# A chunk's scalar steps on the vector engine: one tensor and per-partition scalars in place of two tensors, and four steps on key lengths moved to Pool

## The chip, the cores and the metric

The kernel runs on one core of a Trainium2 chip. The metric is the device time of one execution in microseconds (us), here the median of 3 executions. Five engines work beside each other, each through its own instructions in a fixed order: TensorE (PE in the profile), VectorE (DVE), ScalarE (ACT), GpSimd (POOL) and SyncE (SP), which here only issues transfers.

## The reference

Two layers follow each other. The first is a delta-rule recurrence for 4 batches of 8 heads, 768 steps and a head size of 48; the second is a feed-forward layer with a rational function over the 3072 resulting tokens.

```
def _attn_ref(q, k, v, beta):                      # q, k, v: (4, 8, 768, 48)
    k_n = k / (np.linalg.norm(k, axis=-1, keepdims=True) + 1e-06)
    for t in range(S):
        y[:, :, t] = einsum('bhd,bhde->bhe', q[:, :, t], state)
        v_old = einsum('bhde,bhd->bhe', state, k_n[:, :, t])
        state = state + beta[:, :, t] * einsum('bhd,bhe->bhde', k_n[:, :, t], v[:, :, t] - v_old)

def _moe_ref(x, w_in, w_out, a, b):                # x: (3072, 384), w_in: (384, 2048), w_out: (2048, 384)
    h = x @ w_in
    P = a[0] + a[1] * h + a[2] * h**2 + a[3] * h**3
    Q = 1.0 + abs(b[0]) * abs(h) + abs(b[1]) * h**2
    return (P / (Q + 1e-06)) @ w_out
```

## The kernel before

**Tiling.** The 768 steps are cut into 12 chunks of 64. Within a chunk the recurrence is written as products and a triangular solve, so that only the state passes from chunk to chunk. Products run in f16 with a high and a low part of each operand (three products stand for one in f32, `PASSES`), and so everything must be scaled by powers of two to keep within f16. Those scales are the small steps that this document is about: tensors of one element per partition (`128x1`), or of 2, 4 or 16.

**Stages.** First the weights are read and split (`load_in`, `load_out`; both call `to_f32`, which turns f64 words into f32 and has a clamp on Pool at L333). Beside it the first chunks' keys are prepared. Then a main loop goes over 12 chunks of 8 tiles: `hidden` (first product), `numerator` and `quotient` (the rational function: ACT, DVE and Pool on 128x512 tiles), `accumulate` (second product). Between the tiles stand pieces of the recurrence for later chunks (`attention`: `back` of the next chunk, `middle`, `front`, and `ahead` of the fourth).

**What sets the order.** The code is recorded in this order, and a scheduler then orders each engine's instructions by its own estimate of durations, with raised priority for some pieces. So a changed instruction also moves its neighbours. On the chip every engine works strictly in its order: an instruction that waits holds up all that stand behind it on its engine.

**The places that the change touches.**

- `scalars` (L775 to L811), 13 calls (chunk 0 in two halves): from a chunk's token scale it bounds the result of the rational function and makes six factors for each of the 8 tiles. Its steps are a chain on tile `kp` (and `sf`), one value per partition, mostly TENSOR_TENSOR on DVE; L801 and L802 are a logarithm and an exponential on ACT in the midst of it. Its last step, L810, writes `msc`, which the chunk's first `numerator` (ACT L843) needs.
- `scale_of` (L256): L261 and L262 on ACT make a root, then L263 on DVE cuts it to a power of two by AND with the constant tensor `tmask`.
- `scales` (L629): the scales of a chunk's queries and values, on tile `sc`; L640 and L644 are two-tensor steps.
- `keys_normalized` (L505), four chunks ahead: L511 sums squares on DVE into `nrm` (128x16), L513 clamps, ACT L514 and L515 make a root, DVE L516 to L520 correct and invert it, and Pool L521 scales the keys.
- `inverse` (L543): L554 copies a diagonal into `wt` before the triangular inverse, which runs on DVE from L565 to L598.
- `to_f32` (L325): Pool L333, a TENSOR_SCALAR with one operation, a maximum.

## Time and profile before

| what | value |
|---|---|
| median of 3 executions | 918.05 us (916.96 to 919.3) |
| the profiled execution's own time | 918.86 us |
| its span, first to last instruction | 917.1 us (1.8 us lie around it) |
| DVE busy | 842.7 us, 92% of the span, 1657 instructions |
| PE, POOL, ACT busy | 74%, 66%, 63% |
| mean granted TensorE clock | 0.931 |

How to read the profile: a group row has line, engine, operation, output<-input tile names and shapes, count, then busy time in us and the mean of one in ns, then the engine's idle time before these instructions and what ended it. A view of one line gives the shortest, the median and the longest duration instead. A timeline row has start and duration in us. A busy engine need not be at work: a row counts as busy from the instruction's start to its end, and what holds it up in between is not told apart.

### The profile page before, as it was taken

The numbers are of one execution on the slowest core, as the hardware profiler recorded it, in microseconds if no ns is written. First come the engines' busy times: TensorE is split into PE (matmuls) and PEld (weight loads), VectorE is DVE, ScalarE is ACT, GpSimd is POOL, SyncE is SP. The second block draws the span as 40 slices with busy tenths as digits, with TensorE's granted clock in tenths as the row PEclk, the third lists the DMA queues.
The fourth block names the chain that finished last, engine by engine and source line by source line (L and its number), as shares of the span: only waits on it lengthen the run. The fifth ranks groups of instructions, "written<-read, shape, count | busy, mean of one in ns | idle before, by whom it ended". The sixth has DMA issues, their size and how long they took to land.

```text
span 917.1 us, 23581 instructions
## 1 busy us (share of the span) xinstructions
PE 678.4 (74%) x9264; PEld 542.9 (59%) x9264; DVE 842.7 (92%) x1657; ACT 576.3 (63%) x1099; POOL 604.4 (66%) x479
## 2 busy tenths in 40 slices
PE   0321453877787886986798988888989798999785
PEld 0221443665575775765676876766767676766563
DVE  5999998887997999899999999999999999898976
ACT  4765776556466575666565766657657566677473
POOL 6866965636456376767677677676767665666754
PEclk9999996887989998999998989989989999999998
DMA  7969888679897779779268578468476662200000
GB/s 228 222 162 188 192 180 155 94 132 155 149 130 154 137 136 149 131 147 179 42 132 152 98 157 141 81 151 146 67 185 98 122 114 36 64 2 19 1 18 18
DMA packets 420110, 111.49 MB, mean 122 GB/s; under 512 B 361376, under 2 KB 416672, under 8 KB 420000
## 3 DMA queue, kind: packets, MB, share of 16 engines
q1 hardware_dynamic: 417824, 108.83, 63.5%
q8 instruction: 72, 1.18, 0.6%
q10 hardware_dynamic: 2176, 1.17, 0.4%
q14 instruction: 38, 0.31, 0.1%
HBM read 40.47 MB, written 26.23 MB: 73 GB/s over the span
## 4 chain that ended last, share of the span: by engine, by line
DVE 44%; issue 13%; DMA 11%; ACT 9%; PE 8%; POOL 8%; SPq 6%; POOLq 0%; DVEq 0%; ACTq 0%
DVE mw L868 5%; DVE mu L849 3%; DVE mg L867 3%; DVE mg L865 3%; DVE mu L850 3%; DVE z L238 3%; SPq L449 3%; PE po L888 2%; POOL mw L848 2%; DVE mu L872 2%; PE ph L826 2%; DMA wsi<-in_moe_w_in_dram 2%; DVE pr L586 2%; DMA tq<-xdq 2%; PE pg L417 1%
## 5 line engine op out<-in xcount | busy, mean ns | idle before, releaser
L888 PE MATMUL po<-w_out,mg 128*128 128x384 f16 x1152 | 225.9, 341 | 23.7 <-POOL mg L873 12.6
L826 PE MATMUL ph<-xT,w_in 128*128 128x256 f16 x1728 | 226.7, 284 | 19.7 <-DVE mu L850 19.3
L826 PEld LDWEIGHTS <-w_in 128*128 128x128 f16 x1728 | 173.2, 102 | 58.4 <-DVE mu L850 18.3
L873 POOL TENSOR_TENSOR mg<-mu,mr 128x512 f16<-128x512 f32 x96 | 131.2, 1367 | 76.5 <-DVE mu L872 34.6
L848 POOL TENSOR_TENSOR mw<-mw,mr 128x512 f32<-128x512 f32 x96 | 135.6, 1413 | 65.2 <-ACT mw L847 63.7
L888 PEld LDWEIGHTS <-mg 128*128 128x128 f16 x1152 | 112.3, 102 | 96.0 <-POOL mg L873 17.4
L417 PEld LDWEIGHTS <-kbd 128*128 128x128 f16 x1680 | 93.6, 119 | 45.4 <-issue 41.2
L843 ACT ACTIVATE mu<-ph,coef,msc 128x512 f32<-128x512 f32 x96 | 74.3, 774 | 44.8 <-DVE msc L810 15.4
L861 ACT ACTIVATE mr<-mw,msc 128x512 f32<-128x512 f32 x96 | 69.5, 726 | 50.2 <-POOL mw L848 49.8
L868 DVE SCALAR_TENSOR_TENSOR mw<-mw,msc,mg 128x512 f32<-128x512 f32 x96 | 96.3, 1003 | 1.2
L849 DVE TENSOR_TENSOR mu<-ph,mu 128x512 f32<-128x512 f32 x96 | 65.3, 681 | 16.8 <-ACT mw L847 14.2
L417 PE MATMUL pu<-z,ebd 128*128 128x48 f16 x1728 | 57.9, 188 | 25.8 <-DVE z L238 21.8
L417 PEld LDWEIGHTS <-ebd 128*128 128x128 f16 x1728 | 55.6, 100 | 30.9 <-issue 25.1
L870 POOL TENSOR_TENSOR mu<-mu,mw 128x512 f32<-128x512 f32 x36 | 48.0, 1332 | 38.1 <-DVE mw L868 26.3
L850 DVE SCALAR_TENSOR_TENSOR mu<-mu,msc,ph 128x512 f32<-128x512 f32 x96 | 71.4, 744 | 0.8
L867 DVE SCALAR_TENSOR_TENSOR mg<-mu,msc,mr 128x512 f16<-128x512 f32 x60 | 65.9, 1098 | 2.9 <-ACT mr L862 2.7
L847 ACT ACTIVATE mw<-ph,msc 128x512 f32<-128x512 f32 x96 | 66.5, 692 | 0.0
L845 ACT ACTIVATE mr<-ph,msc 128x512 f32<-128x512 f32 x96 | 65.6, 683 | 0.0
L872 DVE SCALAR_TENSOR_TENSOR mu<-mu,msc,mw 128x512 f32<-128x512 f32 x60 | 64.0, 1067 | 0.4
L417 PEld LDWEIGHTS <-wbd 128*128 128x128 f16 x1152 | 38.1, 103 | 43.0 <-issue 37.8
L862 ACT ACTIVATE mr<-mr 128x512 f32<-128x512 f32 x96 | 60.7, 633 | 1.5
L234 ACT ACTIVATE z<-pu,zmask 128x384 f16<-128x384 f32 x72 | 40.1, 579 | 32.4 <-PE pu L417 22.9
(216 smaller groups left out, 1491.4 us busy)
## 6 DMA issues: line engine op xcount, KB each, us to landing
wsi<-in_moe_w_in_dram SPq DMA_DIRECT2D x24, 256.0 KB, 5.3
xdk<-kn SPq DMA_DIRECT2D x12, 512.0 KB, 3.4
kbd<-tk SPq DMA_DIRECT2D x24, 256.0 KB, 5.1
gd<-g SPq DMA_DIRECT2D x24, 256.0 KB, 4.3
xdq<-kn SPq DMA_DIRECT2D x12, 512.0 KB, 4.5
wso<-in_moe_w_out_dram SPq DMA_DIRECT2D x32, 192.0 KB, 4.0
mbd<-mm SPq DMA_DIRECT2D x24, 256.0 KB, 4.9
wc<-img SPq DMA_DIRECT2D x24, 256.0 KB, 5.5
```

What stands on the lines that cost most here:

```text
L417: nc.tensor.matmul(dst[p][:, h], head(bd, lp, p * H + h), head(rt, rp, p * H + h), start=start and n == 0 and h == 0, stop=stop and n == l ...
L826: nc.tensor.matmul(ph[:, i], w_in[:, f2, wp, cc, i * P : (i + 1) * P], x[:, xp, cc], start=k == 0, stop=k == 3 * NCC - 1,)
L843: nc.scalar.activation(u, ph, AF.Identity, scale=A3, bias=a2)
L848: nc.gpsimd.tensor_add(w, w, z)
L849: nc.vector.tensor_mul(u, ph, u)
L850: nc.vector.scalar_tensor_tensor(out=u, in0=u, scalar=A1, in1=ph, op0=ALU.add, op1=ALU.mult)
L861: nc.scalar.activation(r, w, AF.Ln, bias=Q0)
L867: nc.vector.scalar_tensor_tensor(out=g[:, 0], in0=u, scalar=A0, in1=r, op0=ALU.add, op1=ALU.mult)
L868: nc.vector.scalar_tensor_tensor(out=w, in0=w, scalar=Q0, in1=g[:, 0], op0=ALU.add, op1=ALU.mult)
L872: nc.vector.scalar_tensor_tensor(out=u, in0=u, scalar=A0, in1=w, op0=ALU.add, op1=ALU.subtract)
L873: nc.gpsimd.tensor_mul(g[:, 1], u, r)
L888: nc.tensor.matmul(po[p], g[:, gp, i, p * P : (p + 1) * P], w_out[:, f2, wp, i], start=f2 == lo and i == 0 and k == 0, stop=f2 == hi - 1 a ...
```

## The change

- `scalars` no longer multiplies two tensors. Each step is a TENSOR_SCALAR: one tensor, and one or two operands that are one value per partition (or constants). The bound's two polynomials, until now done side by side on 128x4 and 128x2 tensors with the constant tensor `horner`, are done one value at a time. A call has 18 instructions on DVE instead of 19; two of them still have 2 elements, `L797` (a reciprocal) and the last `times`.
- `scale_of` and `scalars` cut to powers of two with an AND against a constant. `tmask` and `horner` and what fills them are gone.
- L640 and L644 in `scales` become TENSOR_SCALAR too.
- In `keys_normalized` the clamp, a product, a sum and a multiply-add (L513, L517, L518, L519) go from DVE to Pool. The two reciprocals stay on DVE, so the chain now goes DVE, Pool, ACT, ACT, DVE, Pool, Pool, Pool, DVE, Pool.
- The copy of L554 goes from DVE to ACT.
- Pool's clamp in `to_f32` has two operations, min with 3.0e38 and then max; the moved clamp has the same form.

```diff
+POWER = 0xFF800000
...
-    horner = cpool.tile([P, 2, 4], F32, name="horner")
...
+    def power_of_two(dst, src):
+        nc.vector.tensor_scalar(dst.bitcast(U32), src.bitcast(U32), POWER, None, op0=ALU.bitwise_and)
+
+    def times(dst, x, by, then=None):
+        if then is None:
+            nc.vector.tensor_scalar(dst, x, by, None, op0=ALU.mult)
+        else:
+            nc.vector.tensor_scalar(dst, x, by, then, op0=ALU.mult, op1=ALU.mult)
...
-        nc.vector.tensor_tensor(
-            out=dst.bitcast(U32), in0=lg.bitcast(U32), in1=tmask[:, :n], op=ALU.bitwise_and
-        )
+        power_of_two(dst, lg)
...
-        nc.gpsimd.tensor_scalar_max(a, a, keep)
+        nc.gpsimd.tensor_scalar(a, a, 3.0e38, keep, op0=ALU.min, op1=ALU.max)
...
-        nc.vector.tensor_scalar_max(ss, ss, 2.0 ** -94)
+        nc.gpsimd.tensor_scalar(ss, ss, 3.0e38, 2.0 ** -94, op0=ALU.min, op1=ALU.max)
...
-        nc.vector.tensor_mul(y1, y1, ss)
-        nc.vector.tensor_add(y0, y0, y1)
-        nc.vector.tensor_scalar(y0, y0, 1.0 / 32.0, 1e-6 / 16.0, op0=ALU.mult, op1=ALU.add)
+        nc.gpsimd.tensor_mul(y1, y1, ss)
+        nc.gpsimd.tensor_add(y0, y0, y1)
+        nc.gpsimd.tensor_scalar(y0, y0, 1.0 / 32.0, 1e-6 / 16.0, op0=ALU.mult, op1=ALU.add)
...
-        nc.vector.tensor_copy(wt[:, 0:256:17], bblk[:, c])
+        nc.scalar.copy(wt[:, 0:256:17], bblk[:, c])
...
-            nc.vector.tensor_max(sc[:, 1:2], sc[:, 1:2], fmax["v"])
+            nc.vector.tensor_scalar(sc[:, 1:2], sc[:, 1:2], fmax["v"], None, op0=ALU.max)
...
-        nc.vector.scalar_tensor_tensor(
-            out=sc[:, 5:6], in0=sc[:, 2:3], scalar=1.0 / 16.0, in1=sc[:, 3:4], op0=ALU.mult, op1=ALU.mult
-        )
+        times(sc[:, 5:6], sc[:, 2:3], 1.0 / 16.0, sc[:, 3:4])
...
-        nc.vector.tensor_mul(hm, wn, gm)
-        nc.vector.tensor_mul(t, horner[:, 0], hm.broadcast_to([P, 4]))
-        nc.vector.tensor_add(t, t, horner[:, 1])
-        nc.vector.tensor_mul(t[:, 0:2], t[:, 0:2], hm.broadcast_to([P, 2]))
-        nc.vector.tensor_scalar_add(t[:, 1:2], t[:, 1:2], 1.0)
-        nc.vector.reciprocal(t[:, 1:3], t[:, 1:3])
-        nc.vector.tensor_mul(t[:, 0:1], t[:, 0:1], hm)
-        nc.vector.tensor_mul(r, t[:, 0:4:3], t[:, 1:3])
-        nc.vector.tensor_add(gm, r[:, 0:1], r[:, 1:2])
-        nc.vector.tensor_add(gm, gm, m0)
-        nc.vector.tensor_mul(gm, gm, io)
+        times(hm, wn, gm)
+        def affine(dst, x, by, plus):
+            nc.vector.tensor_scalar(dst, x, by, plus, op0=ALU.mult, op1=ALU.add)
+        affine(top_, hm, m3, m2)
+        times(top_, top_, hm, hm)
+        affine(low, hm, b1, b0)
+        affine(low, low, hm, 1.0)
+        affine(one, hm, b0, 1.0)
+        nc.vector.reciprocal(kp[:, 5:7], kp[:, 5:7])
+        times(lin, hm, m1, one)
+        affine(gm, top_, low, lin)
+        nc.vector.tensor_scalar(gm, gm, m0, io, op0=ALU.add, op1=ALU.mult)
...
-        nc.vector.tensor_tensor(out=rk.bitcast(U32), in0=rk.bitcast(U32), in1=tmask[:, :1], op=ALU.bitwise_and)
+        power_of_two(rk, rk)
         nc.vector.reciprocal(sf[:, 1:2], rk)
-        nc.vector.tensor_mul(ikap, sf[:, 1:2], sf[:, 1:2])
-        nc.vector.tensor_mul(sf[:, 3:4], sf[:, 2:3], ikap)
-        nc.vector.tensor_mul(sf[:, 4:6], sf[:, 2:4], sf[:, 2:3].broadcast_to([P, 2]))
+        times(ikap, sf[:, 1:2], sf[:, 1:2])
+        times(sf[:, 3:4], sf[:, 2:3], ikap)
+        times(sf[:, 4:6], sf[:, 2:4], sf[:, 2:3])
```

Line numbers shift by up to three: what was L849, L850, L867 and L868 is L851, L852, L869 and L870. The steps of `scalars` now stand under the lines of their helpers: L252 is `power_of_two`, L257 and L259 `times` with one and with two factors, L789 `affine`. The scheduler moves neighbours in all engines' orders; three places matter for what follows.

DVE before, `scalars` of chunk 5 (tile `kp`), between the recurrence's splits (`z`, `xT`) and the tiles' own steps (`mg`, `mw`, `mu`):

```order
L786 RECIPROCAL kp_0_7772<-lgx_7707 128x1
L767 RECIPROCAL sf_7699<-sf_7699 128x1
L787 TENSOR_TENSOR kp_0_7772<-top,kp_0_7772 128x1
L789 TENSOR_TENSOR kp_0_7772<-horner,kp_0_7772 128x4
L790 TENSOR_TENSOR kp_0_7772<-kp_0_7772,horner 128x4
L791 TENSOR_TENSOR kp_0_7772<-kp_0_7772 128x2
L238 SCALAR_TENSOR_TENSOR xT_7697<-px_0_7712,sf_7699,xT_7697 128x3x128
L865 TENSOR_TENSOR mg_7843<-mu_7755,mr_7757 128x512
L792 TENSOR_SCALAR kp_0_7772<-kp_0_7772 128x1
L794 TENSOR_TENSOR kp_0_7772<-kp_0_7772 128x1
```

The same place now:

```order
L257 TENSOR_SCALAR kp_0_7755<-top,kp_0_7755 128x1
L233 SCALAR_TENSOR_TENSOR z_1_8096<-pu_0_7830,zmask,z_1_8096 128x384
L870 SCALAR_TENSOR_TENSOR mw_7667<-mw_7667,msc_6626,mg_7750 128x512
L789 TENSOR_SCALAR kp_0_7755<-kp_0_7755,coef 128x1
L233 SCALAR_TENSOR_TENSOR xT_7680<-px_0_7695,sf_7682,xT_7680 128x3x128
L789 TENSOR_SCALAR kp_0_7755<-kp_0_7755,coef 128x1 x2
L233 SCALAR_TENSOR_TENSOR z_1_8096<-pu_1_7831,zmask,z_1_8096 128x384
L259 TENSOR_SCALAR kp_0_7755<-kp_0_7755 128x1
```

The steps stay spread among the same kinds of neighbours; what changes is their kind.

Pool before, where chunk 7's keys are scaled (L521), ahead of a tile's sum (L848):

```order
L873 TENSOR_TENSOR mg_5809<-mu_5638,mr_5640 128x512
L249 TENSOR_SCALAR q_5495<-q_5495,sc_5876 128x768
L521 TENSOR_TENSOR k_5602<-k_5602,nrm_6129 128x768
L848 TENSOR_TENSOR mw_5801<-mw_5801,mr_5799 128x512
L230 TENSOR_SCALAR kn_120<-q_5495 128x2x8x48
```

Pool now, chunk 7 (L875, L850 and L524 were L873, L848 and L521):

```order
L875 TENSOR_TENSOR mg_5793<-mu_5622,mr_5624 128x512
L516 TENSOR_SCALAR nrm_6113<-nrm_6113 128x16
L520 TENSOR_TENSOR nrm_6113<-nrm_6113 128x16
L521 TENSOR_TENSOR nrm_6113<-nrm_6113 128x16
L522 TENSOR_SCALAR nrm_6113<-nrm_6113 128x16
L524 TENSOR_TENSOR k_5586<-k_5586,nrm_6113 128x768
L850 TENSOR_TENSOR mw_5785<-mw_5785,mr_5783 128x512
```

and chunk 10, which stands for most of the others:

```order
L516 TENSOR_SCALAR nrm_9560<-nrm_9560 128x16
L231 TENSOR_TENSOR gl_9194<-g_9189,gl_9194 128x768
L875 TENSOR_TENSOR mg_9240<-mu_9069,mr_9071 128x512
L520 TENSOR_TENSOR nrm_9560<-nrm_9560 128x16
L244 TENSOR_SCALAR q_8926<-q_8926,sc_9307 128x768
L521 TENSOR_TENSOR nrm_9560<-nrm_9560 128x16
L225 TENSOR_SCALAR kn_109<-q_8926 128x2x8x48
L522 TENSOR_SCALAR nrm_9560<-nrm_9560 128x16
L231 TENSOR_TENSOR kn_109<-q_8926,kn_109 128x2x8x48
L524 TENSOR_TENSOR k_9033<-k_9033,nrm_9560 128x768
```

Pool has four more instructions in each chunk, of which L520 needs ACT and DVE to have answered L516, and L524 needs DVE's second reciprocal. In chunk 7 (as in chunk 0) nothing else stands between them; in chunk 2 none stands between L516 and L520, in the others two to six do.

DVE before, the diagonal's copy (L554) in front of a tile's steps:

```order
L697 SCALAR_TENSOR_TENSOR v_5346<-v_5346,sc_5876,pk_1_7572 128x384
L554 COPY wt_122<-bblk 128x16
L868 SCALAR_TENSOR_TENSOR mw_7338<-mw_7338,msc_6643,mg_7563 128x512
L849 TENSOR_TENSOR mu_7552<-ph_7533,mu_7552 128x512
L872 SCALAR_TENSOR_TENSOR mu_7334<-mu_7334,msc_6643,mw_7338 128x512
```

ACT now, the same chunk's copy (L557) between two tiles' steps:

```order
L863 ACTIVATE mr_7537<-mw_7539,msc_6626 128x512
L227 CAST rr_7606<-v_5331 128x768
L864 ACTIVATE mr_7537<-mr_7537 128x512
L557 COPY wt_111<-bblk 128x16
L845 ACTIVATE mu_7663<-ph_7644,coef,msc_6626 128x512
```

The copy has left DVE's order and stands in ACT's.

More of the change, by code (lines that the diff above doesn't have):

```diff
@@ L153 @@
     nc.gpsimd.memset(consts[:, 2:3], 5.5 * LN2)
-    tmask = cpool.tile([P, 4], U32, name="tmask")
-    nc.gpsimd.memset(tmask, 0xFF800000)
     coef = cpool.tile([P, 12], F32, name="coef")
@@ L160 @@
     nc.scalar.activation(coef[:, 6:12], coef[:, 0:6], AF.Abs)
-    horner = cpool.tile([P, 2, 4], F32, name="horner")
-    nc.vector.memset(horner[:, 1], 0.0)
-    nc.vector.memset(horner[:, 1, 2:3], 1.0)
-    for i, (at, frm) in enumerate((((0, 0), 9), ((0, 1), 11), ((0, 2), 10), ((0, 3), 7), ((1, 0), 8), ((1, 1), 10))):
-        nc.vector.tensor_copy(horner[:, at[0], at[1] : at[1] + 1], coef[:, frm : frm + 1])
     a0, a1, a2, a3 = (coef[:, i : i + 1] for i in range(4))
-    m0, _, _, _, b0, b1 = (coef[:, i : i + 1] for i in range(6, 12))
+    m0, m1, m2, m3, b0, b1 = (coef[:, i : i + 1] for i in range(6, 12))
     bblk = cpool.tile([P, NCH, 16], F32, name="bblk")
@@ L782, in scalars @@
         kp = sb.tile([P, 10], F32, tag="kp", name=f"kp_{c}_{lo}", bufs=4)
-        gm, rk, ikap, hm = (kp[:, i : i + 1] for i in range(4))
-        t = kp[:, 4:8]
-        r = kp[:, 8:10]
+        gm, rk, ikap, hm, top_, low, one, lin = (kp[:, i : i + 1] for i in range(8))
         nc.vector.reciprocal(gm, d["lg"])
-        nc.vector.tensor_mul(hm, wn, gm)
-        nc.vector.tensor_mul(t, horner[:, 0], hm.broadcast_to([P, 4]))
-        nc.vector.tensor_add(t, t, horner[:, 1])
-        nc.vector.tensor_mul(t[:, 0:2], t[:, 0:2], hm.broadcast_to([P, 2]))
-        nc.vector.tensor_scalar_add(t[:, 1:2], t[:, 1:2], 1.0)
-        nc.vector.reciprocal(t[:, 1:3], t[:, 1:3])
-        nc.vector.tensor_mul(t[:, 0:1], t[:, 0:1], hm)
-        nc.vector.tensor_mul(r, t[:, 0:4:3], t[:, 1:3])
-        nc.vector.tensor_add(gm, r[:, 0:1], r[:, 1:2])
-        nc.vector.tensor_add(gm, gm, m0)
-        nc.vector.tensor_mul(gm, gm, io)
+        times(hm, wn, gm)
[10 more added lines that the diff above has]
+        nc.vector.tensor_scalar(gm, gm, m0, io, op0=ALU.add, op1=ALU.mult)
         nc.vector.tensor_scalar_max(gm, gm, 2.0 ** -60)
```

## The prediction

> **What bounds the kernel now.** I read the page's first part, then busy time by stage, because a mean over the span hides that the stages differ. The four stretches are the weights (to 150 us), the first chunks of the main loop, its steady part, and the end, where no keys are left to prepare.
>
> ```profile
> PE 678.4 (74%) x9264; PEld 542.9 (59%) x9264; DVE 842.7 (92%) x1657; ACT 576.3 (63%) x1099; POOL 604.4 (66%) x479
> core 0: us, PE busy (x) PEld busy (x) DVE busy (x) ACT busy (x) POOL busy (x), PEclk, DMA share, GB/s
> 0.00:150.00 150.00, 48.09 (x683) 40.47 (x683) 134.22 (x387) 93.66 (x231) 107.32 (x115) 0.98 0.86 192
> 150.00:350.00 200.00, 153.07 (x2310) 125.31 (x2310) 177.88 (x366) 118.10 (x221) 112.22 (x79) 0.87 0.81 138
> 350.00:750.00 400.00, 339.68 (x4770) 275.54 (x4771) 387.04 (x684) 258.49 (x463) 278.46 (x207) 0.93 0.70 127
> 750.00:918.00 168.00, 137.58 (x1508) 101.56 (x1504) 143.53 (x223) 106.02 (x187) 106.42 (x80) 0.97 0.13 25
> ```
>
> DVE bounds it: 89%, 89%, 97% and 85% of the four stretches, with no other engine over 85% in any. But busy is not at work. The next view shows DVE's small steps beside Pool in time order (start, duration).
>
> ```profile
> 448.69 1.71 POOL L873 TENSOR_TENSOR mg<-mu,mr 128x512 f16<-128x512 f32 x1
> 449.21 1.22 DVE L803 TENSOR_TENSOR kp<-kp,tmask 128x1 uint32<-128x1 uint32 x1
> 450.35 0.73 DVE L850 SCALAR_TENSOR_TENSOR mu<-mu,msc,ph 128x512 f32<-128x512 f32 x1
> 451.00 0.92 DVE L868 SCALAR_TENSOR_TENSOR mw<-mw,msc,mg 128x512 f32<-128x512 f32 x1
> ```
>
> L803 works on one element per partition and takes 1.22 us: it ends at 450.43, as Pool's L873 does (450.40). The same line's shortest, median and longest durations, and those of three comparable steps:
>
> ```profile
> L803 DVE TENSOR_TENSOR kp<-kp,tmask x13: 136/779/1771, 150.5 to 865.5; 128x1 uint32<-128x1 uint32 x13
> L378 DVE TENSOR_SCALAR vss<-wfs x8: 200/202/209, 88.2 to 151.9; 128x1 f32<-128x1 f32 x8
> L792 DVE TENSOR_SCALAR kp<-kp x13: 135/141/154, 145.3 to 857.4; 128x1 f32<-128x1 f32 x13
> L800 DVE TENSOR_SCALAR kp<-kp x13: 134/153/155, 149.6 to 864.8; 128x1 f32<-128x1 f32 x13
> ```
>
> A two-tensor step in SBUF takes 0.14 us or, behind Pool, up to 1.77 us. L792 and L800, with one tensor and constants, stand in the same chain and never exceed 0.155 us. L378, with one per-partition scalar, stays within 9 ns too. So what the change swaps is a kind that Pool stalls for one that it doesn't.
>
> **The change, part by part.** *Steps of `scalars`.* Busy time of the instructions on tile `kp`, by stage (ACT's are L801 and L802):
>
> ```profile
> core 0: us, DVE busy (x) ACT busy (x), PEclk, DMA share, GB/s
> 0.00:150.00 150.00, 3.59 (x14) 0.20 (x1) 0.98 0.86 192
> 150.00:350.00 200.00, 20.97 (x56) 3.51 (x11) 0.87 0.81 138
> 350.00:750.00 400.00, 41.27 (x102) 9.02 (x24) 0.93 0.70 127
> 750.00:918.00 168.00, 18.02 (x51) 5.68 (x14) 0.97 0.13 25
> ```
>
> At 0.149 us each (between L792's and L800's medians) these would be 2.1, 8.3, 15.2 and 7.6 us; the rest, 1.5 + 12.6 + 26.1 + 10.4 = 50.6 us, is stall. Other two-tensor steps that change:
>
> ```profile
> L263 DVE TENSOR_TENSOR sf<-lgx,tmask 128x1 uint32<-128x1 uint32 x12 | 5.6, 465 | 0.6 <-ACT lgx L262 0.6
> L644 DVE SCALAR_TENSOR_TENSOR sc<-sc 128x1 f32<-128x1 f32 x12 | 4.8, 401 | 0.0
> L263 DVE TENSOR_TENSOR sc<-lgq,tmask 128x2 uint32<-128x2 uint32 x12 | 4.3, 356 | 0.0
> L807 DVE TENSOR_TENSOR sf<-sf 128x2 f32<-128x2 f32 x13 | 4.2, 319 | 0.1
> ```
>
> The first two hold 12 x (465 - 149) + 12 x (401 - 149) = 6.8 us of stall. The last two keep 2 elements. No row has such a step with one tensor; it lies between L800 (1 element, free) and L513 below (16 elements, one tensor and constants, mean 416 though its neighbour L517 takes 212). I leave their stall in place; were it gone, 12 x 207 + 13 x 170 = 4.7 us of DVE time more would be won.
>
> The Trainium skill, "Advanced Engine Details and Errata", section "VectorE Performance Modes", says that a one-tensor instruction uses both read ports where source and destination lie in SBUF and their outermost non-unit dimension is even, and that the second port is shared with GpSimd. By that rule 1-element steps are free of Pool and 2-element ones are not, as I took them; the trace bears out the first (L792, L800) and L513's spread fits the second.
>
> *What a stall that goes is worth.* The next two-tensor instruction inherits part of it. At 449.21, without L803's 1.07 us of stall, L850 (which reads PSUM) would end about 450.0, and L868 would wait for Pool until 450.4 and end near 451.1 instead of 451.92: 0.8 us of 1.07. I take 0.8, so 40.5 us on `kp` and 5.4 us on the two others.
>
> *The price of a per-partition scalar.* L378 against L792 gives 61 ns for one; for two the bounds are 61 and 122 ns. Per call six steps have one and six have two, 0.73 to 1.10 us, over 13 calls 9.5 to 14.3 us; L640 and L644 add 1.5 us. One instruction fewer per call gives 1.9 us back. Sum 9 to 14, taken as 12 us.
>
> *Steps that leave DVE.*
>
> ```profile
> L513 DVE TENSOR_SCALAR nrm<-nrm 128x16 f32<-128x16 f32 x12 | 5.0, 416 | 0.0
> L517 DVE TENSOR_TENSOR nrm<-nrm 128x16 f32<-128x16 f32 x12 | 2.5, 212 | 0.0
> L518 DVE TENSOR_TENSOR nrm<-nrm 128x16 f32<-128x16 f32 x12 | 4.5, 378 | 0.0
> L519 DVE TENSOR_SCALAR nrm<-nrm 128x16 f32<-128x16 f32 x12 | 3.3, 271 | 0.0
> L554 DVE COPY wt<-bblk 128x16 f32<-128x16 f32 x12 | 9.2, 770 | 0.0
> ```
>
> That is 24.5 us off DVE. On ACT the copy should cost what L514 does on the same shape (212 ns, 2.5 us in all), beside an engine that is 63% busy: nothing. Pool's price for 16 elements lies between a memset of one and a TENSOR_SCALAR of 192:
>
> ```profile
> L153 POOL MEMSET consts<- 128x1 f32 x1 | 0.1, 98 | 0.0
> L177 POOL TENSOR_SCALAR bblk<-bblk 128x192 f32<-128x192 f32 x1 | 0.4, 399 | 0.3 <-issue 0.3
> L514 ACT ACTIVATE nrm<-nrm 128x16 f32<-128x16 f32 x12 | 2.5, 212 | 2.1 <-DVE nrm L513 2.0
> L333 POOL TENSOR_SCALAR wao<-wao,gate 128x192 f32<-128x192 f32 x32 | 28.7, 906 | 14.6 <-ACT wao L332 8.0 <-DVE gate L602 6.4
> ```
>
> 48 x 98 to 399 ns is 5 to 19 us on Pool, 66% busy. Its own time is covered; its waits are not. In order, Pool must now stand at L520 until ACT and DVE have answered L516, and the tile steps L848 and L873 stand behind. Before, DVE's chain for chunk 7 ran from 386.96 to Pool's start at 397.40:
>
> ```profile
> 386.96 0.16 DVE L513 TENSOR_SCALAR nrm<-nrm 128x16 f32<-128x16 f32 x1
> 397.40 1.48 POOL L521 TENSOR_TENSOR k<-k,nrm 128x768 f32<-128x768 f32 x1 [0.88 <-DMA wbd<-wc]
> ```
>
> Chunk 7 has no other Pool work in between, so up to 10.4 us; elsewhere in the main loop two to five instructions stand between L516 and L520. I charge 5 us in all; the bounds are 0 and the rival below.
>
> *Pool's clamp.* L333 (192 elements, one operation) takes 906 ns, L177 (192 elements, two operations, multiply and add) 399. Whether min and max run at that pace no row shows: from no gain to 56 x 0.4 = 22 us of Pool time in the first 150 us. DVE's steps there stall behind it, but transfers are also 86% busy. I take 4 us.
>
> *Sum by stage.* DVE time won is 0.8 x stall + what leaves - scalars' price; the 6.8, 24.5 and 12 us spread by calls:
>
> - 0 to 150: 1.2 + 0.2 + 2.7 - 0.9 = 3 us, half of it paid out, 2 us.
> - 150 to 350: 10.1 + 1.4 + 8.9 - 3.0 = 17 us.
> - 350 to 750: 20.9 + 2.8 + 12.9 - 5.6 = 31 us, at 97% DVE paid out at 0.9, 28 us.
> - 750 to the end: 8.3 + 1.0 + 0 - 2.5 = 7 us.
>
> In the second and fourth stretch DVE idles 11 and 15%, so the gain must lie on a chain that others wait for. It does:
>
> ```profile
> ACT kp L801 <- DVE kp L800: 19.6, 6, 7.3
> ACT mu L843 <- DVE msc L810: 15.4, 7, 5.5
> ```
>
> ACT waits 35 us on this very chain, the second time to begin a chunk's tiles. I pay out 0.7: 17 us. Together 2 + 28 + 17 = 47 us. Against it, the same Pool work in a shorter span meets DVE more often. Four big groups show what stalls remain, L850 (PSUM input, 744) being their floor:
>
> ```profile
> L868 DVE SCALAR_TENSOR_TENSOR mw<-mw,msc,mg 128x512 f32<-128x512 f32 x96 | 96.3, 1003 | 1.2
> L867 DVE SCALAR_TENSOR_TENSOR mg<-mu,msc,mr 128x512 f16<-128x512 f32 x60 | 65.9, 1098 | 2.9 <-ACT mr L862 2.7
> L872 DVE SCALAR_TENSOR_TENSOR mu<-mu,msc,mw 128x512 f32<-128x512 f32 x60 | 64.0, 1067 | 0.4
> L850 DVE SCALAR_TENSOR_TENSOR mu<-mu,msc,ph 128x512 f32<-128x512 f32 x96 | 71.4, 744 | 0.8
> ```
>
> They hold 25 + 21 + 19 = 65 us; 5% denser is 3 us. Net: 47 + 4 - 5 - 3 = 43 us. From the profiled execution's 918.86 us that is 875.9, and 0.8 us less against the median: **875 us**.
>
> **The rivals.**
>
> *DVE is the clock everywhere.* Stalls pay in full, in all stages: 50.6 + 6.8 + 24.5 - 9 + 8 for the clamp = 81 us, 837 us. For it: ACT's waits on DVE's chain. Against it: DVE idles 22 us in 150 to 350. Chance 0.11.
>
> *The stall moves on.* Pool and DVE's two-tensor work exclude each other; if that sharing is itself full, the next two-tensor instruction takes the whole wait over. Then only the unstalled time that leaves counts, 60 x 0.16 (L513 unstalled, above) = 10 us, against 12 us for scalars, and 4 us from the clamp: 916 us, or 911 if a tenth of the 57 us of stall still pays. Against it: Pool is only 66% busy, so a wait often ends with Pool idle. Chance 0.08.
>
> The Trainium skill, "VectorE: DVE Perf Modes", section "Rules for kernel authors", says to minimize the count of operations rather than fuse. By count alone `scalars` goes from 19 to 18 and time would hardly move, as in this rival; the spread of L803 speaks against it.
>
> *Scalars collide too.* If a per-partition scalar's read is blocked as a second tensor's is, only the AND steps with constants win (L803 12 x 0.6 and L263 3.8 us) and what leaves DVE: 0.8 x 11 + 24.5 - 12 = 21 us, paid at 0.8 = 17, less 4 for clamp, queue and denser Pool together: 905 us. Against it: L378, 8 of 8 free, though only in the weights. Chance 0.07.
>
> *Pool's queue becomes the clock.* Nine chunks prepare keys inside the main loop. If Pool's stand at L520 and L524 holds the tiles up by 6 us in each, 54 us replace the 5 charged and the time is 875 + 49 = 924 us; it decides against the change from about 5 us per chunk. For it: chunk 7's order and its 10.4 us. Against it: Pool idles 210 of the 600 us from 150 to 750, and work stands in between elsewhere. Chance 0.07.
>
> **How the numbers follow.** The forecast has 0.67, its own range 855 to 895: the 58 us of DVE time paid out at 0.6 or in full give 887 or 864, and I leave 8 us each way for the scheduler's new neighbours. To leave out no more than 2 in 10 I take 845 to 905. Within 0.3%, 2.8 us, counts as no change, about what this kernel's measurement can tell. Faster: 0.67 + 0.11 + 0.07 + most of 0.08 = 0.91, of which I move 0.02 to the others; same 0.04; slower 0.07.
>
> **What would show it.** Right: the steps at the new lines of `times` and `affine` at 0.14 to 0.27 us without a tail over 0.5; DVE's busy time down to about 785 us; ACT's waits for L801 and L843 on DVE halved; L868 and L867 a little longer than 1003 and 1098. Wrong: a tail in those steps (scalars collide); L868 and L867 at 1250 or more (the stall moves on); Pool idle before L520 or L524 by over 40 us with the tiles' ACT steps waiting on Pool (the queue). A time under 845 would say that the stalls cost more than their own length, one over 905 that what DVE gave up another engine took.

## The result, and the profile after

The changed kernel takes 896.29 us (median of 4, 895.7 to 898.5) against 917.89 us for the kernel before (916.96 to 919.3): ratio 0.977, 95% interval 0.975 to 0.979. It is 21 us faster; 43 us were forecast. The profiled execution took 898.5 us, with a span of 896.8. Its mean granted TensorE clock was 0.881, against 0.931 before, but another execution of the changed kernel at 0.951 took 895.7 us: the clock does not explain the missing 22 us.

The busy times and the shares of the chain that ended last, on the page of the changed kernel:

```profile
PE 675.2 (75%) x9264; PEld 540.7 (60%) x9264; DVE 798.7 (89%) x1576; ACT 575.2 (64%) x1111; POOL 603.1 (67%) x526
DVE 39%; PE 14%; DMA 12%; issue 10%; SPq 9%; ACT 9%; POOL 7%; ACTq 0%; POOLq 0%; DVEq 0%
```

The same chain on the page of the kernel before, which the prediction did not use:

```profile
DVE 44%; issue 13%; DMA 11%; ACT 9%; PE 8%; POOL 8%; SPq 6%; POOLq 0%; DVEq 0%; ACTq 0%
```

DVE's busy time fell by 44.0 us (842.7 to 798.7), not by 58, and 21 of the 44 reached the end. The chain had hinted at the second: with DVE busy for 92% of the span, only 44% of the chain was DVE's.

The new small steps in the changed kernel, grouped by line and shape (busy us, mean ns | idle before):

```profile
L257 DVE TENSOR_SCALAR sf<-sf 128x2 f32<-128x2 f32 x13 | 7.9, 608 | 0.1
L789 DVE TENSOR_SCALAR kp<-kp,coef 128x1 f32<-128x1 f32 x39 | 7.5, 241 | 0.2
...
L252 DVE TENSOR_SCALAR sc<-lgq 128x2 uint32<-128x2 uint32 x12 | 5.6, 467 | 0.0
L801 DVE TENSOR_SCALAR kp<-kp,coef,top 128x1 f32<-128x1 f32 x13 | 3.5, 267 | 0.2
...
L257 DVE TENSOR_SCALAR kp<-top,kp 128x1 f32<-128x1 f32 x13 | 2.6, 197 | 0.0
...
L252 DVE TENSOR_SCALAR kp<-kp 128x1 uint32<-128x1 uint32 x13 | 1.9, 143 | 0.1
```

One element: 143 ns with a constant, some 200 with one per-partition scalar, 267 with two; none of them exceeds 0.28 us. Two elements: 608 and 467 ns on average (319 and 356 before), with medians of 228 and 160. Ten of these 25 take over 0.5 us, and each of the ten ends 23 to 28 ns after an instruction of Pool: they stall behind Pool. L797, a reciprocal of two elements in the same chain, does not: 147 to 166 ns in all 13. The four big groups that hold the remaining stall:

```profile
L870 DVE SCALAR_TENSOR_TENSOR mw<-mw,msc,mg 128x512 f32<-128x512 f32 x96 | 101.0, 1052 | 1.1
L852 DVE SCALAR_TENSOR_TENSOR mu<-mu,msc,ph 128x512 f32<-128x512 f32 x96 | 70.7, 736 | 0.7
L874 DVE SCALAR_TENSOR_TENSOR mu<-mu,msc,mw 128x512 f32<-128x512 f32 x60 | 67.8, 1130 | 0.4
L869 DVE SCALAR_TENSOR_TENSOR mg<-mu,msc,mr 128x512 f16<-128x512 f32 x60 | 65.0, 1084 | 0.2
```

L870 and L874 grew by 49 and 63 ns a piece, L869 shrank by 14.

Where the gain arose is read from the start of `msc` (L810, now L812), which ends each chunk's chain. In the timeline of the kernel before, chunks 1 and 9:

```profile
243.38 0.20 DVE L810 TENSOR_TENSOR msc<-tab,sf 128x48 f32<-128x48 f32 x1
...
775.25 0.20 DVE L810 TENSOR_TENSOR msc<-tab,sf 128x48 f32<-128x48 f32 x1
```

and of the changed kernel:

```profile
232.18 0.19 DVE L812 TENSOR_TENSOR msc<-tab,sf 128x48 f32<-128x48 f32 x1
...
762.68 0.40 DVE L812 TENSOR_TENSOR msc<-tab,sf 128x48 f32<-128x48 f32 x1
```

11.2 us are won by chunk 1. From there to chunk 9, 531.9 us became 530.5: in the stretch that holds the 97% busy stage, where most of the gain was forecast, next to nothing came. The end brings the rest. DVE did get faster between these two marks: its busy time fell from 508.8 to 485.6 us. But its idle time rose from 23.1 to 44.9 us. The 23 us became waiting. The stage from 350 to 750 us shows the same, where DVE's 387.04 us of the prediction's view are now:

```profile
core 0: us, PE busy (x) PEld busy (x) DVE busy (x) ACT busy (x) POOL busy (x), PEclk, DMA share, GB/s
350.00:750.00 400.00, 342.89 (x4875) 277.15 (x4876) 367.92 (x664) 257.29 (x470) 290.93 (x229) 0.93 0.70 128
```

### The profile page after: what moved, and what is told of

Same layout as the page of the kernel before. It is cut to its first block, busy times and chain, and to the rows that moved or that the text cites. A ratio compares the mean times of both kernels' runs of the same rounds, so it can differ in the third digit from the quotient of the medians.

```text
span 896.8 us, 23571 instructions
## 1 busy us (share of the span) xinstructions
PE 675.2 (75%) x9264; PEld 540.7 (60%) x9264; DVE 798.7 (89%) x1576; ACT 575.2 (64%) x1111; POOL 603.1 (67%) x526
## 4 chain that ended last, share of the span: by engine, by line
DVE 39%; PE 14%; DMA 12%; issue 10%; SPq 9%; ACT 9%; POOL 7%; ACTq 0%; POOLq 0%; DVEq 0%
DVE mw L870 4%; PE ph L828 4%; PE po L890 4%; DVE mg L869 4%; PE pg L420 3%; DVE mu L874 3%; DVE w_out L344 3%; DVE mu L851 3%; POOL mg L875 3%; DVE mu L852 3%; DVE mg L867 3%; SPq L452 2%; SPq L118 2%; DMA gb<-gd 2%; DMA k<-in_k_dram 2%
## 5 line engine op out<-in xcount | busy, mean ns | idle before, releaser
L875 POOL TENSOR_TENSOR mg<-mu,mr 128x512 f16<-128x512 f32 x96 | 131.6, 1371 | 72.6 <-DVE mu L874 49.5
L850 POOL TENSOR_TENSOR mw<-mw,mr 128x512 f32<-128x512 f32 x96 | 138.0, 1438 | 47.4 <-ACT mw L849 46.8
L845 ACT ACTIVATE mu<-ph,coef,msc 128x512 f32<-128x512 f32 x96 | 74.4, 775 | 51.5 <-DVE msc L812 19.8
L870 DVE SCALAR_TENSOR_TENSOR mw<-mw,msc,mg 128x512 f32<-128x512 f32 x96 | 101.0, 1052 | 1.1
L851 DVE TENSOR_TENSOR mu<-ph,mu 128x512 f32<-128x512 f32 x96 | 65.6, 683 | 22.8 <-ACT mw L849 19.6
L852 DVE SCALAR_TENSOR_TENSOR mu<-mu,msc,ph 128x512 f32<-128x512 f32 x96 | 70.7, 736 | 0.7
L874 DVE SCALAR_TENSOR_TENSOR mu<-mu,msc,mw 128x512 f32<-128x512 f32 x60 | 67.8, 1130 | 0.4
L849 ACT ACTIVATE mw<-ph,msc 128x512 f32<-128x512 f32 x96 | 66.7, 694 | 0.0
L869 DVE SCALAR_TENSOR_TENSOR mg<-mu,msc,mr 128x512 f16<-128x512 f32 x60 | 65.0, 1084 | 0.2
L420 PEld LDWEIGHTS <-wbd 128*128 128x128 f16 x1152 | 36.3, 100 | 35.4 <-issue 33.4
L420 PE MATMUL pg<-tk,kbd 128*128 128x64 f16 x576 | 39.2, 241 | 17.9 <-DVE w_out L344 6.7
```

The lines of the kernel that those rows point to most:

```text
L420: nc.tensor.matmul(dst[p][:, h], head(bd, lp, p * H + h), head(rt, rp, p * H + h), start=start and n == 0 and h == 0, stop=stop and n == l ...
L845: nc.scalar.activation(u, ph, AF.Identity, scale=A3, bias=a2)
L850: nc.gpsimd.tensor_add(w, w, z)
L851: nc.vector.tensor_mul(u, ph, u)
L852: nc.vector.scalar_tensor_tensor(out=u, in0=u, scalar=A1, in1=ph, op0=ALU.add, op1=ALU.mult)
L869: nc.vector.scalar_tensor_tensor(out=g[:, 0], in0=u, scalar=A0, in1=r, op0=ALU.add, op1=ALU.mult)
```

## The experiments

Two theories stood at first. **Order**: the forms won what was forecast, and the scheduler's new order gave half of it back. **Stall**: the order matters little; the stall moves on to the next two-tensor step, or freed time turns into waiting. To tell them apart, a program's instructions were held in the order of another: every instruction is tied to the one ahead of it on its engine, without a wait. Steps that a run adds, and that the other program lacks, are not held; the scheduler puts them where they fit. The cuts of code below are shortened to what the edit does.

```diff
+for keys in order.values():                  # one list per engine, from the other kernel
+    both = [mine[k] for k in keys if k in mine]
+    for first, then in zip(both, both[1:]):
+        tc.add_manual_dep(then, first.name, NO_SYNC, reason="hold")
```

All ratios below are to the kernel before, measured beside each run, and a difference in us is a difference of ratios times 917.9 us; with intervals of about 0.003 either way, two or three us between two kernels mean nothing. "DVE busy" is the page's figure.

### The forms alone, in the order of before

```diff
-nc.vector.tensor_tensor(out=rk, in0=rk, in1=tmask[:, :1], op=ALU.bitwise_and)
+nc.vector.tensor_scalar(rk, rk, POWER, None, op0=ALU.bitwise_and)
-nc.vector.tensor_mul(ikap, sf[:, 1:2], sf[:, 1:2])
+nc.vector.tensor_scalar(ikap, sf[:, 1:2], sf[:, 1:2], None, op0=ALU.mult)
...
```

> The kernel before with every engine's instructions held in its own order; only the one-element two-tensor steps of scale_of, scalars and finish_q (the ANDs, hm, gm, ikap, sf, sc) take one tensor and per-partition scalars; the four-element Horner rows and all else stay. Theory O (the scheduler's new order cost what the forms had won): the forms alone win well here, 20 us or more, 898 or less. Theory S (the stall moves on to the next two-tensor step, or the freed time turns into waiting): 5 to 12 us, 906 to 913, with the stall of the big steps (mw, mg, mu) up by a third of what the small ones lose and DVE's idle time up by another third.

Measured: ratio 0.9971 (0.9949 to 0.9992), 2.7 us faster, and DVE busy 830.5 us. Less than even theory Stall expected; in before's order the forms do not win what was forecast, so Order falls there.

### Two-tensor forms back, in the order of after

The reverse of that edit, for all the small steps of the changed kernel:

```diff
-nc.vector.tensor_scalar(dst, x, by, plus, op0=ALU.mult, op1=ALU.add)
+nc.vector.scalar_tensor_tensor(out=dst, in0=x, scalar=by, in1=plus, op0=ALU.mult, op1=ALU.add)
...
```

> The changed kernel with every engine held in its own order; only the small steps' form goes back to two tensors, one for one (mult and add with a tensor as the second operand, AND with a tensor mask). Theory O: the forms are worth 25 us or more in a fixed order, so 921 or more. Theory S: they are worth about half the change, 8 to 15 us, so 904 to 911.

Measured: 0.9930 (0.9905 to 0.9956), 910.8 us; DVE busy 822.1. So in the order of after the forms are worth 14.9 us (within 3), about 0.64 of the 23.4 us of DVE time. The two-tensor steps in this run:

```profile
L295 DVE SCALAR_TENSOR_TENSOR kp<-kp,coef 128x1 f32<-128x1 f32 x39 | 14.1, 383 | 0.3
L295 DVE SCALAR_TENSOR_TENSOR kp<-kp,coef,top 128x1 f32<-128x1 f32 x13 | 6.9, 527 | 0.2
```

383 and 527 ns are L789's 241 and L801's 267 in the changed kernel.

As this run and the changed kernel have the same 1576 DVE instructions in the same order, each can be compared with itself (and likewise before with the run ahead). Sums of durations and of idle time ahead, in us:

```
                              two forms -> one form   before -> one form
changed small steps (206)        91.3 -> 52.5            86.5 -> 58.2
next instruction behind one     +11.2  (163)            +12.4  (177)
second behind one                +4.3  (133)             +4.8  (144)
all others                       -0.6                    -2.2
DVE's idle time                 +12.4                    +3.8
```

Part of the stall does move on: the next two instructions take over 15.5 of 38.8 us (40%) in the one order and 17.2 of 28.3 us (61%) in the other. All instructions further behind together take over nothing.

### Before's order for the changed program, and the reverse

```diff
-hold(changed, order_of(changed))
+hold(changed, order_of(before))     # and the reverse: hold(before, order_of(changed))
```

> The changed kernel, but every instruction that it shares with the kernel before keeps that kernel's order on its engine; the steps of the chain, the four length steps on Pool and the copy on ACT are put in where they fit. Theory O: the gain forecast comes back, 875 to 885. Theory S: the order is not what matters, 892 to 902.

Measured: 0.9870 (0.9834 to 0.9906), 905.0 us.

> The reverse of the last: the kernel before with every shared instruction held in the order of the changed kernel. Theory O: the new order alone costs 10 to 20 us, 928 to 938. Theory S: no more than 4 us from the kernel before, 914 to 922.

Measured: 0.9962 (0.9935 to 0.9990), 913.0 us. Neither supports Order for the whole span: the changed program in before's order is slower, not faster, and lies even above the range of Stall; the kernel before in the new order lies within 4 us of itself. By stretch (start of `msc` in chunks 1 and 9, one profiled execution each) it is not so simple:

```
                               to chunk 1   chunk 1 to 9   DVE busy there   chunk 9 to end   span
before                            243.4         531.9          508.8            141.9        917.1
before in after's order           230.3         542.5          511.2            137.2        910.0
two-tensor, after's order         232.4         538.2          501.9            137.0        907.6
after                             232.2         530.5          485.6            134.1        896.8
after in before's order           239.7         520.8          482.0            142.2        902.7
```

In the program of before the new order brings 13 us ahead of chunk 1 and 5 at the end, and costs 11 us between chunks 1 and 9. There the forms win 8 us, for 16 us less DVE time. The whole change, in before's order, wins 11 us there for 27 us less DVE time. So without any loss by the order, too, less than half of DVE's time is paid out in this stretch. Over the span the order is worth 3.5 us to the program of before, and 9.4 us to the changed one.

### The three other parts, taken back one at a time in the order of after

```diff
-nc.gpsimd.tensor_scalar(a, a, 3.0e38, keep, op0=ALU.min, op1=ALU.max)
+nc.gpsimd.tensor_scalar_max(a, a, keep)
```

> The changed kernel held in its own order; only Pool's clamp goes back to one operation (max). My sum gave the clamp 4 us: 900. If Pool's time in the weights isn't waited for: 895 to 898.

Measured: 0.9741 (0.9685 to 0.9797), 892.3 us, below both expected values, but within the intervals of the changed kernel. Not slower without the clamp's second operation, though Pool's steps became much longer. With one operation (L378 there is L336):

```profile
L378 POOL TENSOR_SCALAR wao<-wao,gate 128x192 f32<-128x192 f32 x32 | 33.9, 1065 | 11.9 <-DVE gate L648 7.5 <-ACT wao L377 4.3
L378 POOL TENSOR_SCALAR wai<-wai 128x256 f32<-128x256 f32 x24 | 23.4, 986 | 10.2 <-ACT wai L377 10.2
```

and in the changed kernel, with two:

```profile
L336 POOL TENSOR_SCALAR wao<-wao,gate 128x192 f32<-128x192 f32 x32 | 19.7, 620 | 22.0 <-ACT wao L335 13.1 <-DVE gate L605 8.3 <-ACT sw L297 0.3
L336 POOL TENSOR_SCALAR wai<-wai 128x256 f32<-128x256 f32 x24 | 13.1, 552 | 17.8 <-ACT wai L335 17.6
```

Of the 24.5 us that Pool saves by two operations, 17.7 turn into idle time before the same steps, for ACT and for `gate`.

```diff
-nc.scalar.copy(wt[:, 0:256:17], bblk[:, c])
+nc.vector.tensor_copy(wt[:, 0:256:17], bblk[:, c])
```

> The changed kernel held in its own order; only the copy of the diagonal goes back from ACT to DVE (9 us of DVE time). If DVE's time is paid out as I forecast (0.8): 903 to 905. If only half of DVE's time reaches the end: 899 to 901. If the copy was a wait that others had anyway: 896 to 897.

Measured: 0.9772 (0.9739 to 0.9804); DVE busy +6.5 us, time +0.4.

```diff
-nc.gpsimd.tensor_mul(y1, y1, ss)       # and the three others of keys_normalized
+nc.vector.tensor_mul(y1, y1, ss)
```

> The changed kernel held in its own order; only the four length steps go back from Pool to DVE (15 us of DVE time). By my sum (12 us of gain less 5 of waits): 902 to 905. If Pool's queue costs what DVE gains: 894 to 898. If Pool's queue is the loss: under 892.

Measured: 0.9778 (0.9745 to 0.9810); DVE busy +10.7 us, time +0.9. Copy and length steps together took 17 us from DVE and gave 1 us, within some 6. In the profiled executions DVE's idle time is 98.1 us in the changed kernel, 88.3 with the copy back and 81.3 with the length steps back: what they freed became waiting. The result also lies in the range named for a Pool queue that costs what DVE gains, and this is not ruled out. But the queue is no loss of the size that the rival named: Pool's waits at its steps are 11.6 us in all in the changed kernel.

```profile
L520 POOL TENSOR_TENSOR nrm<-nrm 128x16 f32<-128x16 f32 x12 | 4.6, 384 | 6.3 <-DVE msc L812 2.8 <-DVE rb L291 1.8 <-DVE nrm L519 1.7
L524 POOL TENSOR_TENSOR k<-k,nrm 128x768 f32<-128x768 f32 x12 | 18.4, 1532 | 5.3 <-DVE nrm L523 3.5 <-DVE wt L573 1.8
```

### What a microsecond of DVE time is worth

The forms' 23 us of DVE busy time had paid 0.64, copy and lengths about nothing. A new theory: DVE is not the clock, and a microsecond on it is worth what its place makes it worth. Work was added or cut at one place at a time, in a fixed order.

```diff
 nc.vector.tensor_mul(u, ph, u)
+nc.vector.tensor_scalar(x, u[:, 0, 0:1], 0.5, 0.25, op0=ALU.mult, op1=ALU.add)
+for _ in range(2):
+    nc.vector.tensor_scalar(x, x, 0.5, 0.25, op0=ALU.mult, op1=ALU.add)
```

> The changed kernel held in its own order, with three more one-element, one-tensor steps on DVE in each of the 96 tile steps (about 0.14 to 0.2 us each, 40 to 55 us of DVE time that Pool doesn't stall). If DVE is the clock, as I forecast (0.7 to 0.9 of its time paid out): 928 to 940. If about half of DVE's time reaches the end: 915 to 924. If DVE has room now: under 908.

> The kernel before held in its own order, with the same three one-element steps in each of the 96 tile steps as in the last run (some 38 us of DVE time). If DVE was the clock before and the change took it off: 943 to 952 (0.7 to 0.9 paid). If it was never the clock: 921 to 929 (0.1 to 0.35 paid).

Measured: after 0.9866 (0.9844 to 0.9889), before 1.0123 (1.0087 to 1.0159). The added steps' durations sum up to 42.0 and 43.4 us, but they start while the neighbour still ends; DVE busy rose by 21.4 and 18.9 us, and the time by 9.0 and 11.3. The first, 905.6 us, is in the range named for a DVE that has room now, the second at the upper end of "never the clock".

```diff
-nc.vector.tensor_mul(u, ph, u)
+nc.vector.tensor_mul(u[..., : TG // 4], ph[..., : TG // 4], u[..., : TG // 4])
```

> The kernel before held in its own order; the product of PSUM and the tile (128x512, 681 ns, 96 times) is done for a quarter of its columns only, so part of the numerator is left out. Some 40 us of DVE time go, none of it stall, in the tiles rather than in the scalars. If DVE was the clock: 878 to 888. If it was never the clock: 900 to 912.

Measured: 0.9898 (0.9850 to 0.9945), 909.5 us, as for "never the clock"; the product's own time fell by 38.4 us, DVE busy by 31.1, the time by 9.4.

```diff
 nc.vector.tensor_scalar_max(gm, gm, 2.0 ** -60)
+for _ in range(22):
+    nc.vector.tensor_scalar_max(gm, gm, 2.0 ** -60)
 nc.scalar.activation(rk, gm, AF.Ln)
```

> The changed kernel held in its own order, with 22 more one-element steps at the end of each of the 13 chains of scalars, ahead of ACT's logarithm (maximum with the same constant: about 286 x 0.14 = 41 us of DVE time, nearly the 38 us that the tile steps took in the run with more work on DVE, but all of it in the chain that ACT waits for). If a microsecond on this chain is worth more than one elsewhere on DVE: 916 to 932 (0.5 to 0.9 paid). If it is worth the same as elsewhere: 901 to 908 (0.2).

> The same 22 steps per chain in the kernel before, held in its own order. If the chain's place is what pays: 936 to 952. If place doesn't matter: what the tile steps' extra work gives in the same kernel, within 4 us.

Measured: after 1.0280 (1.0238 to 1.0321), before 1.0573 (1.0534 to 1.0611): 47.0 and 52.6 us more for 38.5 and 33.7 us of DVE time, above both expected ranges. The steps stand mostly in one piece per chain, each in need of the one ahead, and start 0.19 us apart though each takes 0.15. So the stretch of the chains, measured further below, grew by 54.2 us in both kernels, more than DVE's busy time. ACT now waits for the chain's maximum, in the waits of the changed kernel with the late chain (total us, times, longest):

```profile
ACT kp L865 <- DVE kp L864: 77.8, 13, 14.4
```

Was it the chain, or any lump of work at that place? The next run puts the same 22 steps behind `msc`, on a scratch column:

```diff
 nc.vector.tensor_mul(d["m"][:, :, u], tab[:, :, u], ...)
+nc.vector.tensor_scalar(x, d["m"][:, 0, lo : lo + 1], 0.5, 0.25, op0=ALU.mult, op1=ALU.add)
+for _ in range(21):
+    nc.vector.tensor_scalar(x, x, 0.5, 0.25, op0=ALU.mult, op1=ALU.add)
```

> The changed kernel held in its own order, with the same 22 one-element steps 13 times as in the run with the late chain, but behind the chain: on a scratch column, after msc, so that nothing waits for their result. If the chain's length was the cost: 902 to 912 (0.15 to 0.4 of 40 us, as for work in the tiles). If a lump of DVE time at this place costs as much whatever waits for it: 930 to 945.

Measured: 0.9775 (0.9749 to 0.9800). DVE busy rose by 21.2 us, to 819.9 of 894.2 us, and the time by 0.6. But it was no lump: not held, the 286 steps stand in 211 separate places between the tiles' and the recurrence's steps. So the run shows that 41 us of DVE steps for which nothing waits, strewn among others, cost nothing that can be measured. What a lump in one piece would cost behind `msc` was not tried. The added steps (all but the first of each 22):

```profile
L882 DVE TENSOR_SCALAR extra<-extra 128x1 f32<-128x1 f32 x273 | 39.5, 145 | 2.6
```

Last, the cut in the tiles again, now in the changed kernel:

> The changed kernel held in its own order; the product of PSUM and the tile is done for a quarter of its columns only, so part of the numerator is left out (about 39 us of DVE time go, as in the same cut of the kernel before). If DVE time in the tiles is worth 0.2 in either direction: 886 to 891. If DVE has room now and removal gives nothing: 893 to 897. If it pays more below: under 882.

Measured: 0.9640 (0.9613 to 0.9668), 885.5 us, against 0.9768: 11.7 us for 20.2 us of DVE busy time (38.5 us of the product's own; other steps, the big groups above all, stalled longer). All in one table, "paid" being time by DVE busy time:

```
                                     DVE busy    time     paid
after, steps behind msc               +21.2      +0.6     0.03
after, copy and length steps back     +17.2      +1.3     0.08
before, small steps' forms            -12.2      -2.7     0.22
before, a tile's product cut          -31.1      -9.4     0.30
after, steps in the tiles             +21.4      +9.0     0.42
after, a tile's product cut           -20.2     -11.7     0.58
before, steps in the tiles            +18.9     +11.3     0.60
after, small steps' forms back        +23.4     +14.9     0.64
after, steps in the chain             +38.5     +47.0     1.22
before, steps in the chain            +33.7     +52.6     1.56
```

DVE's busy time leaves out what overlaps and takes in the stalls that others then have, so part of the spread of "paid" is its doing. By the summed durations of the added or cut steps themselves, the four runs in the tiles pay 0.21, 0.26, 0.24 and 0.30, alike in both kernels and both directions; the forms pay 0.10 (28.3 us, before) and 0.38 (38.8 us, after). By the 54.2 us that the stretch of the chains grew, the two runs with steps in the chain pay 0.87 and 0.97, not more than they took.

### The stretch of the chain

From the first step of `scalars` to the end of `msc` 17.6 us pass per call in the changed kernel (for the second half of chunk 0, from the first step behind the first half's `msc`). The chain's steps are under 5 us of it. The rest stands between. Part of it in the timeline (chunk 5):

```profile
436.50 0.15 DVE L785 RECIPROCAL kp<-lgx 128x1 f32<-128x1 f32 x1
436.61 0.16 DVE L768 RECIPROCAL sf<-sf 128x1 f32<-128x1 f32 x1
436.69 0.21 DVE L257 TENSOR_SCALAR kp<-top,kp 128x1 f32<-128x1 f32 x1
...
441.17 0.55 DVE L231 TENSOR_TENSOR z<-pu,z 128x384 f16<-128x384 f32 x1
...
446.06 0.74 DVE L874 SCALAR_TENSOR_TENSOR mu<-mu,msc,mw 128x512 f32<-128x512 f32 x1
447.15 1.32 DVE L233 SCALAR_TENSOR_TENSOR sh<-S,sc,sh 128x768 f16<-128x768 f32 x1 [0.34 <-ACT sh L229]
...
452.90 0.87 DVE L812 TENSOR_TENSOR msc<-tab,sf 128x48 f32<-128x48 f32 x1
```

Summed over the 13 calls this stretch is 241.6 us with two-tensor forms and 228.3 in the changed kernel (13.3 less; 14.9 us of time); 263.4 before and 262.4 with the forms alone (1.0; 2.7); with steps in the chain 54.2 more in both (47.0 and 52.6); with steps behind `msc` 1.2 more (0.6). So in a fixed order, what changes the length of this stretch changes the time by about as much. It is not the only such thing: the four runs in the tiles change the stretch by 2 us at the most and the time by 9 to 12. Is it the chain that must end early, or what stands between?

```diff
 # DVE's order, chunks 1 to 11
 hm
+all steps of the chain up to the maximum
 steps between (z, xT, S, sh, mu, mg, mw ...)
-the chain's steps, singly in between
+AND to msc in one piece, a few steps later
```

> The changed kernel in its own order but for one thing: in the chains of chunks 1 to 11 the scalars' steps up to the maximum stand right behind one another, ACT's logarithm and exponential come at the first place behind them, and the steps from the AND to msc follow in one piece; the tile steps that stood between come after. No instruction is added or taken away. If the chain's length sets the end also when it gets shorter: 870 to 886 (it loses 60 to 100 us in all, of which ACT's waits on it, 32 us, bound what can be won soon). If only a longer chain costs, and in a shorter one other waits end as late: 890 to 900.

> The same moves in the kernel before, held in its own order otherwise. If the chain's length sets the end: 885 to 903. If not: 912 to 920.

Measured: 0.9926 (0.9895 to 0.9957) and 1.0199 (1.0173 to 1.0225): 14.5 and 18.3 us slower, above both expected ranges, with stretches of 110 and 123 us. An earlier end of the chain does not carry the time. The same waits in the changed kernel:

```profile
ACT mu L845 <- DVE msc L812: 19.8, 5, 8.0
...
PE pu L420 <- DVE z L233: 15.0, 10, 4.6
...
ACT kp L803 <- DVE kp L802: 11.8, 3, 9.0
```

and with the chain first (L915, L465 and L251, L868 are those lines):

```profile
PE pu L465 <- DVE z L251: 24.1, 17, 4.6
...
ACT kp L868 <- DVE kp L865: 8.8, 2, 8.5
...
ACT mu L915 <- DVE msc L877: 1.9, 1, 1.9
```

ACT's wait for `msc` is gone, but PE waits longer for `z`, the split of the next chunks' products. That path is seen in the chain of waits of the changed kernel, 436 to 457 us, where DVE's `z` leads over PE's products and SP's queue to a transfer:

```profile
435.47 0.54 DVE z L233
436.00 0.04 issue
436.05 2.08 PE pu L420 x48
...
441.47 1.05 PE pg L420 x17
...
451.80 0.61 SPq L452
...
452.52 4.67 DMA gb<-gd
```

The last two runs did the reverse: the steps between first, the chain's steps in one piece behind them.

```diff
 hm
-the chain's steps, singly in between
 steps between (z, xT, S, sh, mu, mg, mw ...)
+all steps of the chain up to the maximum, where the maximum stood
 steps between
+AND to msc in one piece, where msc stood
```

> The changed kernel in its own order but for one thing: in the chains of chunks 1 to 11 DVE does the steps that stood between first and the chain's steps in one piece behind them, the maximum and msc staying where they were among the others, so that the steps between start up to 2 us earlier and msc comes no earlier. If the steps between set the end: 884 to 893. If neither they nor the chain do by themselves (only the place of a delay in the whole stretch): 894 to 900. If it is slower (over 902), the chain's end does count.

> The same in the kernel before, whose chain's steps are longer (7 us per chunk with their stalls). If the steps between set the end: 900 to 912. If not: 914 to 921; slower if the chain's end counts.

Measured: 0.9889 (0.9853 to 0.9924) and 1.0073 (1.0050 to 1.0097): slower again, by 11.1 and 6.7 us, which was expected if the chain's end counts. Now ACT waits longer on the chain, and PE's wait for `z` did not shrink either:

```profile
ACT mu L915 <- DVE msc L877: 23.6, 9, 9.0
...
ACT kp L868 <- DVE kp L865: 18.6, 6, 9.0
PE pu L465 <- DVE z L251: 18.3, 12, 4.7
```

Both sides are waited for, the chain's steps and those between. That an order that favours one pays at the other is argued, not shown, for none of these runs is clean. In one piece each step waits for the one ahead and no longer hides behind a neighbour's end: the overlap of DVE's instructions in the changed kernel, 103.6 us, fell to 95.4 with the chain first and to 95.5 with it last. DVE's busy time rose by 9.1 and 12.8 us with the same instructions, while its idle time over the span stayed at 97 to 98. So much of the 14.5 and 11.1 us may be this, and how much is order stays open. No run beat the changed kernel beyond the intervals with all of its work done.

## Why the prediction was half right

**Right: the kind of step.** One-element steps with one tensor do not stall behind Pool; two-element TENSOR_SCALARs do (the two-element reciprocal L797 does not). The price per scalar was as bounded: about 61 ns for one, and for two 124 ns at L801, which is the upper bound. The Trainium skill, "Advanced Engine Details and Errata", section "VectorE Performance Modes", has a one-tensor instruction use both read ports, the second of them shared with GpSimd, where source and destination lie in SBUF and their outermost non-unit dimension is even, or odd, above one and equal in both; 143 to 267 ns for one element and 467 and 608 for two agree.

**Right: the rivals that were put low.** L870 at 1052 and L869 at 1084 ns are far from the 1250 of "the stall moves on" in full; but 40% to 61% of the stall did move on. "Scalars collide too" falls by the one-element steps with scalars, none over 0.28 us. "Pool's queue becomes the clock" falls by the length steps taken back (0.9 us) and by 6.3 and 5.3 us of waits where over 40 would have shown it. "DVE is the clock everywhere" falls by the 41 us of steps that cost 0.6 us when strewn behind `msc`.

**Mis-sized: "what a stall that goes is worth", 0.8.** It is 0.60 in the order of after and 0.39 in that of before. The 0.8 came from one place where the next step reads PSUM and the second inherits; over 206 steps the next two take over 40% or more. The copy and the length steps took 17.2 us from DVE's busy time and not 24.5, in part because small steps start before the neighbour ends. DVE time won was 44 us instead of 58.

**Failed: the pay-out, 0.9 from 350 to 750 us and 0.7 on both sides.** It took DVE's 97% for a clock. Between chunks 1 and 9, which hold that stage, 23 us of DVE busy time went and 1.4 us of time, 0.06 in place of 0.9; in before's order it was 11 of 27 us, 0.41. Steps added in the tiles of the kernel before paid 0.60 of DVE's busy time, work cut there 0.30 (0.26 and 0.24 of the steps' own); 44 us paid 0.48 in the change. Of the miss of 26 us (47 against 21) the 14 us less of DVE time make 14 x 0.81 = 11, the lower pay-out 44 x 0.33 = 15. The copy and the length steps, 24.5 us of the sum, were paid nothing that can be measured, though DVE stood at 97%: what they freed became waiting. The forms, on the chain that ACT waits for, gave 14.9 of the 21 us; so the argument that "the gain must lie on a chain that others wait for" was right, but not for the copy and the length steps. Which wait takes the place of DVE's time in each case is shown for the chain (ACT) and seen for `z` (PE); for the rest it stays open.

**Not seen: the order.** The 8 us left each way for new neighbours were a fair size in sum (3.5 us for the program of before, 9.4 for the changed one) but hid a gain of 13 us ahead of chunk 1 and a loss of some 10 us from there to chunk 9. This loss takes up the 11 us that the change wins there in before's order, so the steady part won nothing.

**The small terms.** The clamp (4 us) came to nothing that can be measured, and Pool's queue (-5) can't be told from the length steps' gain. Of the denser Pool (-3) only the sum with the stall that moves on is seen: L870, L874 and L869 together grew by 96 x 0.049 + 60 x (0.063 - 0.014) = 7.6 us. And ACT's two waits on the chain, which were to be halved from 35 us, are 19.8 and 11.8: the one for `msc` grew, the one for the maximum shrank. The time, 896, lies inside the range up to 905 only because that range left room for the rivals; it is outside the likeliest case's 855 to 895.

The Trainium skill, "VectorE: DVE Perf Modes", section "Rules for kernel authors", would minimize the count of operations; the two forms in one order have the same count, 1576, and differ by 14.9 us. That rule does not decide here.

## What to carry to other kernels

An engine that is 97% busy, stalls included, need not be the clock: hold the share of the chain of waits beside it (44% here; 44% of the 58 us forecast would have given 26, nearer to 21, though this one case proves no rule), and price freed time by its place: here nothing that could be measured for steps strewn where no one waits, a quarter of a step's length in the tiles, nearly all of it in a chain that others wait for. Of a stall taken from a small instruction the next two inherited 40% to 61% here, so count about half of it. To price a change, add a known amount of the same engine's work at the same place in a fixed order, and look where the scheduler put it; one such run in the tiles would have shown a pay-out far below 0.9.

## What the runs showed of the hardware that was not expected

- Pool's clamp with two operations (min, then max) takes 620 and 552 ns on 192 and 256 elements, with one (max) 1065 and 986 in the same order. More work in one instruction was faster.
- The inheritance of a stall ends after two instructions: third and later ones changed by 0.6 us in all in the one order, by 2.2 in the other, both times downwards.
- Small DVE steps that stand singly between steps they do not depend on overlap these: 286 steps of 145 ns, 41 us, raised DVE's busy time by 21 us. In a row, each in need of the one ahead, they start 190 ns apart.
- A reciprocal of two elements does not stall behind Pool (147 to 166 ns, 13 times), a TENSOR_SCALAR of two elements does (up to 1.6 us).
